# Scores of a head pair as two products over 64 rows and two over 3 rows, in place of one widened product per head

## The chip, the cores and the metric

The kernel runs on one core of one Trainium2 chip. Its time is the device time of one execution in microseconds; a kernel's figure is the median of its runs. One execution was also taken by the hardware profiler, and its trace and page are what this document reads. In them TensorE is PE (matmuls) and PEld (the loads of the stationary operand, which overlap the matmuls), VectorE is DVE, ScalarE is ACT, GpSimd is POOL, and SyncE is SP, which issues most DMAs.

## The reference

Attention in which a query sees only the keys whose nearest centroid is its own, followed by a gated feed-forward block:

```python
# q, k, v: (4, 8, 768, 64); centroids: (8, 16, 64)
q_assign = argmax(einsum('bhsd,hcd->bhsc', q_n, c_n), -1)     # q_n, k_n, c_n: of length 1
k_assign = argmax(einsum('bhsd,hcd->bhsc', k_n, c_n), -1)
mask = q_assign[:, :, :, None] == k_assign[:, :, None, :]
scores = where(mask, q @ k.T / 8, -1e9)
x = softmax(scores) @ v                                        # heads joined: (4, 768, 512)
h = maximum(x @ w_in, 0)                                       # (4, 768, 1024)
gate = sigmoid(conv_w[0]*h[s-1] + conv_w[1]*h[s] + conv_w[2]*h[s+1])
out = (h * gate) @ w_out                                       # float32
```

## The kernel before, in words

The work goes by head pairs: a group `g` is one batch and two heads, so there are 16 groups. A group has two units `t` (the first and the second 384 queries), so there are 32 units. For a group, q and k are loaded in float32 and turned so that the 128 partitions hold the two heads' 64 features each (`qkT`): by PE transposes and copies (`T`, `Qa`, `Qd`) for ten groups, by DVE transposes (`D`) for six. `A` (L318) multiplies by the centroids: four products of 32 output columns each, one per quarter of PE's columns, twice over. `M0` to `M6` are the seven DVE steps of the argmax, `K` turns the resulting numbers with a PE transpose (L386), `Bd` or `Ba` copies them out of PSUM, and `BX` sends them by DMA to where the scores read them.

The mask is put into the scores as three extra rows of the product: with u and w the (shifted, sharpened) cluster numbers of key and query, the rows add a term that is 0 where they are equal and very negative where they are not, and the exponential then gives 0. The operand `ext` has, for each head, 64 rows of features, 3 bias rows (`BR`), and zeros up to 128. `zp` and `zd` fill the zeros once for each of the five buffers. Head 1's features lie in partitions 64 to 127 of `qkT` and must get to partitions 0 to 63 of `ext`: for groups 0 to 3 by casts across partitions (`CDa`, `CDp`, `CDd`, 64 rows each), for the others by one cast of 128 rows into `c16` (`CQ`) and two DMAs (`CX`).

A unit has six score steps `S.t.i` (L413): step `i` takes one head and two key tiles of 128, two products of 128x128 by 128x384, into the two PSUM banks of one of two buffers `sc`. The exponential `E.t.i` (L425) reads both banks on ACT in one go. The values `V.t.u` (L444) are 36 products of 65 columns a unit. Then come the normalisation (`NR`, `N`), the turn of x (`X`, `Y`, or `XD` by DMA), and the feed-forward part: `I` (L498), relu `R`, the three taps of the convolution on DVE (`a`, `b`, `c`, L530 and L532), tanh `H` (L560), gate `G` (L569), the output product `O` (L581), and its way out (`F`, `FX`). `_k.n` are n products on zeros ahead of the real work.

The order of everything is written out in one string, `PLAN`; each engine runs its own steps in that order, and an instruction that waits holds up what stands behind it on its engine. The name after `@` is the PSUM bank.

Of the kernel before, what the change touches and what calls it, by code (L numbers as in the profile page):

```python
# [8 lines left out]
F32 = mybir.dt.float32  # L9
# [7 lines left out]
NE = 5  # L17
NHP = 6
NHK = 2
BUFS = {'qk_in': 4, 'qkT': 2, 'c16': 1, 'v_in': 2, 'spk': 2, 'attn': 4, 'x16': 3, 'cnv': 2, 'th': 2, 'hg': 2, 'o_sb': 2, 'w_sb': 1, 'sim': 1, 'eqq': 1, 'val': 1, 'mx': 3, 'best': 3, 'rec': 3}  # L20

PLAN = (
# [842 lines left out]
```

## Time and profile before

| | |
|---|---|
| median of 3 runs | 241.66 us (241.6 to 242.12) |
| the profiled execution | 240.97 us, of which 239.2 us is the span of its instructions |
| PE busy | 228.5 us, 96% |
| PEld busy | 145.5 us, 61% |
| DVE busy | 209.8 us, 88% |
| ACT busy | 209.5 us, 88% |
| POOL busy | 71.0 us, 30% |
| granted TensorE clock | 1.0 in the whole span |

A busy share tells which engine has the least room over the whole span. It does not tell by itself that the engine is the limit, since a matmul's record goes on until its last result is modelled to be written, while the next one has long begun. How close the products follow each other is read from their starts in the timeline.

### The profile page before, as it was taken

The numbers are of one execution on the slowest core, as the hardware profiler recorded it, in microseconds if no ns is written. First come the engines' busy times: TensorE is split into PE (matmuls) and PEld (weight loads), VectorE is DVE, ScalarE is ACT, GpSimd is POOL, SyncE is SP. The second block draws the span as 40 slices with busy tenths as digits, with TensorE's granted clock in tenths as the row PEclk, the third lists the DMA queues.
The fourth block names the chain that finished last, engine by engine and source line by source line (L and its number), as shares of the span: only waits on it lengthen the run. The fifth ranks groups of instructions, "written<-read, shape, count | busy, mean of one in ns | idle before, by whom it ended". The sixth has DMA issues, their size and how long they took to land.

```text
span 239.2 us, 6261 instructions
## 1 busy us (share of the span) xinstructions
PE 228.5 (96%) x2420; PEld 145.5 (61%) x2420; DVE 209.8 (88%) x417; ACT 209.5 (88%) x326; POOL 71.0 (30%) x120
## 2 busy tenths in 40 slices
PE   7889899999999999989999999999999999999993
PEld 6757567676766775645566556655656666665541
DVE  5689677766989999999999999999899999999950
ACT  3757899898999999989999999997999999987841
POOL 7348690974944004360200340007120000000000
PEclk9999999999999999999999999999999999999999
DMA  8966979899995957796578957885491104022233
GB/s 153 217 154 171 292 192 313 268 225 230 267 229 164 192 96 140 111 152 135 154 144 148 133 129 167 197 135 102 110 249 38 33 3 175 4 88 88 90 132 132
DMA packets 97481, 36.79 MB, mean 154 GB/s; under 512 B 88745, under 2 KB 91305, under 8 KB 97452
## 3 DMA queue, kind: packets, MB, share of 16 engines
q1 hardware_dynamic: 96524, 36.17, 66.4%
q8 instruction: 19, 0.31, 0.6%
q10 hardware_dynamic: 928, 0.23, 0.5%
q14 instruction: 10, 0.08, 0.1%
HBM read 23.11 MB, written 6.29 MB: 123 GB/s over the span
## 4 chain that ended last, share of the span: by engine, by line
PE 65%; DVE 24%; issue 4%; DMA 3%; SPq 1%; ACT 1%; DVEq 0%; ACTq 0%
PE sc L413 18%; PE flex L581 12%; PE flex L498 11%; PE flex L444 10%; DVE cnv L532 5%; PE flex L277 4%; DVE hg L569 3%; PE flex L318 3%; PE tail L581 3%; DMA qk_in<-in_k_dram 2%; PE tail L498 2%; DVE sim L342 2%; DVE val L357 2%; DVE qkT L285 2%; DVE hpad L513 1%
## 5 line engine op out<-in xcount | busy, mean ns | idle before, releaser
L425 ACT ACTIVATE attn<-sc 128x768 f16<-128x768 f32 x192 | 148.1, 829 | 8.7 <-PE sc L413 7.4
L413 PE MATMUL sc<-ext 128*128 128x384 f16 x384 | 90.4, 325 | 0.3
L532 DVE SCALAR_TENSOR_TENSOR cnv<-hpad,cwcol,cnv 128x768 f16<-128x768 f16 (+2 forms) x72 | 62.4, 890 | 0.1
L444 PEld LDWEIGHTS <-attn 128*128 128x128 f16 x1152 | 50.9, 97 | 17.3 <-issue 2.7
L444 PE MATMUL flex<-v,attn 128*128 128x65 f16 x1152 | 55.0, 193 | 0.4 <-DVE sim L342 0.4
L498 PE MATMUL flex<-xT,w_in 128*128 128x384 f16 x228 | 45.5, 325 | 0.3 <-DVE x L460 0.2
L235 POOL CAST c<-qkT 128x768 f16<-128x768 f32 x21 | 21.4, 1027 | 76.6 <-DVE qkT L285 22.9
L413 PEld LDWEIGHTS <-ext 128*128 128x128 f16 x384 | 31.3, 97 | 20.4 <-issue 7.9
L581 PE MATMUL flex<-w_out,hg 128*128 128x512 f16 x160 | 42.3, 379 | 0.0
L498 PEld LDWEIGHTS <-w_in 128*128 128x128 f16 x256 | 24.1, 97 | 16.2 <-issue 1.0
L569 DVE SCALAR_TENSOR_TENSOR hg<-th,hpad 128x768 f16<-128x768 f32 (+3 forms) x34 | 31.1, 919 | 0.4 <-ACT th L560 0.3
L581 PEld LDWEIGHTS <-hg 128*128 128x128 f16 x192 | 17.7, 98 | 16.2 <-issue 0.6
L560 ACT ACTIVATE th<-cnv 128x768 f32<-128x768 f16 (+2 forms) x30 | 25.9, 864 | 1.2 <-DVE cnv L532 1.0
L235 POOL CAST v<-v_in 128x768 f16<-128x768 f32 x16 | 15.9, 997 | 18.9 <-DMA v_in<-in_v_dram 14.1
L511 ACT ACTIVATE hpad<-flex 128x384 f16<-128x384 f32 x39 | 19.5, 536 | 0.4 <-PE flex L498 0.4
L277 PE MATMUL flex<-id,qk_in 128*128 128x128 f32 x120 | 17.5, 277 | 1.6 <-DMA qk_in<-in_k_dram 0.9
L460 DVE TENSOR_TENSOR x<-flex,rec 128x384 f16<-128x384 f32 x32 | 17.5, 547 | 0.2
L277 PEld LDWEIGHTS flex<-id,qk_in 128*128 128x128 f32 x120 | 13.4, 141 | 4.0 <-issue 1.1
L318 PE MATMUL flex<-qkT,cT 128*32 128x384 f32 x128 | 13.6, 498 | 1.6 <-DVE qkT L285 0.8
L235 DVE COPY qkT<-flex 128x512 f32<-128x512 f32 x15 | 10.1, 686 | 5.4 <-PE flex L277 5.3
L530 DVE TENSOR_SCALAR cnv<-hpad,cwcol 128x768 f16<-128x768 f16 (+2 forms) x36 | 14.5, 411 | 0.3 <-ACT th L560 0.2
L233 ACT ACTIVATE qkT<-flex 128x512 f32<-128x512 f32 x15 | 8.7, 603 | 5.3 <-PE flex L277 5.3
(81 smaller groups left out, 210.2 us busy)
## 6 DMA issues: line engine op xcount, KB each, us to landing
v_in<-in_v_dram SPq DMA_DIRECT2D x16, 384.0 KB, 4.6
ext<-c SPq DMA_DIRECT2D x24, 192.0 KB, 3.2
out_dram<-o_sb SPq DMA_DIRECT2D x9, 512.0 KB, 2.8
qk_in<-in_q_dram SPq DMA_DIRECT2D x20, 192.0 KB, 3.1
qk_in<-in_k_dram SPq DMA_DIRECT2D x9, 384.0 KB
qk_in<-in_k_dram SPq DMA_DIRECT2D x24, 96.0 KB, 2.3
qk_in<-in_q_dram SPq DMA_DIRECT2D x24, 96.0 KB, 3.8
w_sb<-in_moe_w_in_dram SPq DMA_DIRECT2D x4, 512.0 KB, 4.4
```

Of the source, the lines that this page charges most:

```text
L235: (nc.vector if name == "d" else nc.gpsimd).tensor_copy(out=to, in_=src)
L277: nc.tensor.transpose(bank[at][:, P * i : P * (i + 1)], qk_t[g][:, o, P * j : P * (j + 1)], id128[:])
L318: nc.tensor.matmul(bank[at][32 * j : 32 * (j + 1), 0:HS], lhsT=cT32[:, g % NPR, :], rhs=tokens[:, j], start=True, stop=True, skip_group_ch ...
L413: nc.tensor.matmul(s[:, n, 0:HS], lhsT=ext_b[g % NE][:, h, 1, P * (kt + n) : P * (kt + n + 1)], rhs=ext_b[g % NE][:, h, 0, HS * a : HS * ( ...
L425: nc.scalar.activation(attn[t, i // 3][:, kt : kt + 2, :], sc[(6 * t + i) % 2][:, :, 0:HS], AF.Exp, scale=0.125)
L444: nc.tensor.matmul(avp(at)[:, u, 0 : D + 1], lhsT=attn[t, h][:, kt, P * jq : P * (jq + 1)], rhs=v16_b[g % NE][:, h, kt, 0 : D + 1], start= ...
L498: nc.tensor.matmul(bank[at][:, 0:HS], lhsT=w_in16[:, r, 2 * u + f, :], rhs=xT[:, b % 2, r, HS * a : HS * (a + 1)], start=(r == 0), stop=(r ...
L511: nc.scalar.activation(to, src, AF.Relu)
L532: nc.vector.scalar_tensor_tensor(out=cnv, in0=src, scalar=w, in1=cnv, op0=ALU.mult, op1=ALU.add)
L560: nc.scalar.activation(th, cnv_t[key].rearrange("p (f s) -> p f s", s=N), AF.Tanh, scale=0.5)
L569: nc.vector.scalar_tensor_tensor(out=hg_b[b][:, 2 * u + fs.start : 2 * u + fs.stop, lo : lo + N], in0=th, scalar=1.0, in1=hpad(b, u)[:, fs ...
L581: nc.tensor.matmul(bank[at][:, 0:Dm], lhsT=hg_b[b][:, fb, P * tq : P * (tq + 1)], rhs=w_out16[:, fb, :], start=(fb == 0), stop=(fb == NFB ...
```

## The change

A score step now takes both heads and one key tile. It makes four products: two over 64 rows (head 0 in partitions 0 to 63, head 1 in 64 to 127, where the features already lie), then two over the 3 bias rows that add to the same banks (head 0's bias in partitions 0 to 2, head 1's in 64 to 66). Head 0 goes to the first bank of `sc`, head 1 to the second. The columns that come out and the exponentials are as many as before, but `attn` is now one tile for both heads, so `V.t.0` needs all six exponentials of its unit. The features are cast in one go of 128 rows (`CD`), there are no shifts (`CX`), no zero fills, no argmax of a single head; `BX` goes once for each head, 36 partitions each.

```diff
+    bias_b = [const.tile([P, 2, S], F16, name=f"bias{i}") for i in range(NE)]
-    ext_b = [const.tile([P, 2, 2, S], F16, name=f"ext{i}") for i in range(NE)]
+    ext_b = [const.tile([P, 2, S], F16, name=f"ext{i}") for i in range(NE)]
...
     def cast_qk(name, g, o):
-        copy(name, c_t[g][:, o], qkT[g][:, o])
+        copy(name, ext_b[g % NE][:, o], qkT[g][:, o])
-    def shift_qk(g, h):
-        nc.sync.dma_start(ext_b[g % NE][0:D, h], c_t[g][D * h : D * (h + 1)])
...
     def bias_rows(g, h, queue=nc.sync):
+        to = bias_b[g % NE][D * h : D * h + BR].rearrange("r o s -> r (o s)")
+        queue.dma_start(to, spk_t[g][60 * h : 60 * h + 36, :])
...
-    def scores(t, i):
-        h, kt = i // 3, 2 * (i % 3)
-        for n in range(2):
-            nc.tensor.matmul(
-                s[:, n, 0:HS],
-                lhsT=ext_b[g % NE][:, h, 1, P * (kt + n) : P * (kt + n + 1)],
-                rhs=ext_b[g % NE][:, h, 0, HS * a : HS * (a + 1)],
-                start=True,
-                stop=True,
-            )
+    def scores(t, kt):
+        s = sc[(6 * t + kt) % 2]
+        for x, K, first in ((ext_b, D, True), (bias_b, BR, False)):
+            for h in range(2):
+                rows = slice(D * h, D * h + K)
+                nc.tensor.matmul(
+                    s[:, h, 0:HS],
+                    lhsT=x[g % NE][rows, 1, P * kt : P * (kt + 1)],
+                    rhs=x[g % NE][rows, 0, HS * a : HS * (a + 1)],
+                    start=first,
+                    stop=not first,
+                    skip_group_check=True,
+                )
...
-                lhsT=attn[t, h][:, kt, P * jq : P * (jq + 1)],
+                lhsT=attn[t][:, kt, h, P * jq : P * (jq + 1)],
```

`PLAN` is another one throughout. Counted in it, before and now: `CX` 24 and 0; casts of 128 rows of q or k 24 and 32, casts of 64 rows 16 and 0 (on ACT, both widths together, 4 and 7); `BX` 18 and 32; argmax passes 18 (four of them of half width) and 16; `zp` and `zd` 10 and 0; products of `_k` 113 and 118. `BUFS` now has two `attn` tiles of double size instead of four, and three `o_sb` instead of two.

On PE, in the middle of the work, a score step that is followed by a feed-forward product. Before (`ext` is the widened operand, `sc` the score buffer):

```order
L444 MATMUL flex_66<-v_4_104,attn 128x65
L413 LDWEIGHTS ext_96
L413 MATMUL sc_77<-ext_96 128x384
L413 LDWEIGHTS ext_96
L413 MATMUL sc_77<-ext_96 128x384
L498 LDWEIGHTS w_in_84
L498 MATMUL flex_69<-xT,w_in_84 128x384
```

Now (L359 is the score line, L442 the feed-forward line):

```order
L359 LDWEIGHTS ext_98
L359 MATMUL sc_77<-ext_98 128x384
L359 LDWEIGHTS ext_98
L359 MATMUL sc_77<-ext_98 128x384
L359 LDWEIGHTS bias_103
L359 MATMUL sc_77<-bias_103 128x384
L359 LDWEIGHTS bias_103
L359 MATMUL sc_77<-bias_103 128x384
L442 LDWEIGHTS w_in_84
L442 MATMUL flex_66<-xT,w_in_84 128x384
```

The step went from two weight loads and two products of 384 columns to four of each; the two on `ext` use 64 of PE's rows each, the two on `bias` use 3 each, and what stands around them uses all 128.

On DVE, at the start, the first group's argmax. Before (`sim` holds the products with the centroids, `hpack` the numbers of single heads):

```order
L342 STREAM_TRANSPOSE sim_275<-flex2_68 128x384
L345 TENSOR_REDUCE mx_277<-sim_275 128x12
L345 TENSOR_REDUCE mx_279<-sim_275 128x12
L351 TENSOR_TENSOR eqq_281<-sim_275,mx_277 128x192
L357 TENSOR_TENSOR val_283<-eqq_281,iota16_83 128x192
L361 TENSOR_REDUCE best_285<-val_283 128x12
L351 TENSOR_TENSOR eqq_287<-sim_275,mx_279 128x192
L365 TENSOR_SCALAR hpack0_108<-best_285 128x12
```

Now (`pack0` is that of both heads of group 0):

```order
L310 STREAM_TRANSPOSE sim_216<-flex2_68 128x384
L313 TENSOR_REDUCE mx_276<-sim_216 128x24
L317 TENSOR_TENSOR eqq_278<-sim_216,mx_276 128x384
L321 TENSOR_TENSOR val_280<-eqq_278,iota16_83 128x384
L324 TENSOR_REDUCE best_282<-val_280 128x24
L329 TENSOR_SCALAR pack0_110<-best_282 128x2x12
L333 TENSOR_TENSOR pack0_110<-pack0_110 128x4x6
L231 COPY spk_290<-flex0_66 96x128
L310 STREAM_TRANSPOSE sim_333<-flex3_69 128x384
```

The two half passes of group 0 became one pass over both heads, and group 1's pass follows it at once.

More of the change, by code (lines that the diff above doesn't have):

```diff
@@ L18 @@
 NHP = 6
-NHK = 2
-BUFS = {'qk_in': 4, 'qkT': 2, 'c16': 1, 'v_in': 2, 'spk': 2, 'attn': 4, 'x16': 3, 'cnv': 2, 'th': 2, 'hg': 2, 'o_sb': 2, 'w_sb': 1, 'sim': 1, 'eqq': 1, 'val': 1, 'mx': 3, 'best': 3, 'rec': 3}
+NHK = 0
+BUFS = {'qk_in': 4, 'qkT': 2, 'v_in': 2, 'spk': 2, 'attn': 2, 'x16': 3, 'cnv': 2, 'th': 2, 'hg': 2, 'o_sb': 3, 'w_sb': 1, 'sim': 1, 'eqq': 1, 'val': 1, 'mx': 3, 'best': 3, 'rec': 3}
 PLAN = (
[118 rows of a table removed]
[114 rows of a table added]
 )
@@ L221 @@
     pack_b = [const.tile([P, P], F16, name=f"pack{i}") for i in range(NPK)]
-    hpack_b = [const.tile([P, P], F16, name=f"hpack{i}") for i in range(NHK)]
     hpad_b = [const.tile([P, 2, S + 4], F16, name=f"hpad{i}") for i in range(NHP)]
-    qk_t, v_t, qkT, chunk_at, c_t = {}, {}, {}, {}, {}
+    qk_t, v_t, qkT, chunk_at = {}, {}, {}, {}
     sims_at, sim_t, mx_t, eq_t, val_t, turn_at, spk_t = {}, {}, {}, {}, {}, {}, {}
@@ L285, in block_transpose @@
         nc.vector.transpose(qkT_of(g)[:, o, :], qk_t[g][:, o, :])
-    def cast_direct(name, g, h, o):
-        copy(name, ext_b[g % NE][0:D, h, o], qkT[g][D * h : D * (h + 1), o, :])
     def cast_qk(name, g, o):
-        if g not in c_t:
-            c_t[g] = rot.tile([P, 2, S], F16, name="c16", tag="c16", bufs=BUFS["c16"])
-        copy(name, c_t[g][:, o], qkT[g][:, o])
-    def transfer_cast(g, h):
-        nc.gpsimd.dma_start(ext_b[g % NE][0:D, h], qkT[g][D * h : D * (h + 1)])
-    def load_v_cast(g):
-        b, h0 = batch_pair(g)
-        src = v[b, h0 : h0 + 2]
-        to = v16_b[g % NE].rearrange("p h j w -> p (h j) w")[:, :, 0:D]
-        if KIND[g] == "B":
-            nc.gpsimd.dma_start(to, src.rearrange("h (j p) d -> p (h j) d", p=P))
-        else:
-            for h in range(2):
-                nc.gpsimd.dma_start(to[:, J * h : J * (h + 1)], src[h].rearrange("(p j) d -> p j d", j=J))
-    def shift_qk(g, h):
-        nc.sync.dma_start(ext_b[g % NE][0:D, h], c_t[g][D * h : D * (h + 1)])
+        copy(name, ext_b[g % NE][:, o], qkT[g][:, o])
     def cast_v(name, g):
@@ L325, in assign, with argmax @@
             )
-    def argmax(g, h, i):
-        key = g, h
-        n = 2 if h is None else 1
-        G = 12 * n
-        pack = pack_b[g % NPK] if h is None else hpack_b[g]
+    def argmax(g, i):
+        pack = pack_b[g % NPK]
         def shape(x):
-            return x[:, 0 : G * C].rearrange("p (u h c) -> p u h c", h=n, c=C)
-        def sim():
-            x = sim_t[g].rearrange("p (u h c) -> p u h c", h=2, c=C)
-            return x if h is None else x[:, :, h : h + 1]
+            return x[:, 0 : 24 * C].rearrange("p (u c) -> p u c", c=C)
         if i == 0:
@@ L343, in argmax @@
         elif i == 1:
-            mx_t[key] = rot.tile([P, 24], F32, name="mx", tag="mx", bufs=BUFS["mx"])
-            nc.vector.tensor_reduce(
-                out=mx_t[key][:, 0:G].rearrange("p (u h) -> p u h", h=n), in_=sim(), axis=AX.X, op=ALU.max
-            )
+            mx_t[g] = rot.tile([P, 24], F32, name="mx", tag="mx", bufs=BUFS["mx"])
+            nc.vector.tensor_reduce(out=mx_t[g][:], in_=shape(sim_t[g]), axis=AX.X, op=ALU.max)
         elif i == 2:
-            eq_t[key] = rot.tile([P, 24 * C], F16, name="eqq", tag="eqq", bufs=BUFS["eqq"])
@@ L350, in argmax @@
-            mx = mx_t.pop(key)[:, 0:G].rearrange("p (u h) -> p u h", h=n).unsqueeze(3).to_broadcast((P, 12, n, C))
-            nc.vector.tensor_tensor(out=shape(eq_t[key]), in0=sim(), in1=mx, op=ALU.is_equal)
+            eq_t[g] = rot.tile([P, 24 * C], F16, name="eqq", tag="eqq", bufs=BUFS["eqq"])
+            mx = mx_t.pop(g)[:].unsqueeze(2).to_broadcast((P, 24, C))
+            nc.vector.tensor_tensor(out=shape(eq_t[g]), in0=shape(sim_t[g]), in1=mx, op=ALU.is_equal)
         elif i == 3:
-            val_t[key] = rot.tile([P, 24 * C], F16, name="val", tag="val", bufs=BUFS["val"])
@@ L354, in argmax @@
-            iota = iota16[:].unsqueeze(1).to_broadcast((P, G, C))
-            eq = eq_t.pop(key)[:, 0 : G * C].rearrange("p (u c) -> p u c", c=C)
-            val = val_t[key][:, 0 : G * C].rearrange("p (u c) -> p u c", c=C)
-            nc.vector.tensor_tensor(out=val, in0=eq, in1=iota, op=ALU.mult)
-        elif i == 4:
-            mx_t[key] = rot.tile([P, 24], F32, name="best", tag="best", bufs=BUFS["best"])
-            val = val_t.pop(key)[:, 0 : G * C].rearrange("p (u c) -> p u c", c=C)
-            nc.vector.tensor_reduce(out=mx_t[key][:, 0:G], in_=val, axis=AX.X, op=ALU.max)
-        elif i == 5:
-            best = mx_t.pop(key)[:, 0:G].rearrange("p (u h) -> p h u", h=n)
-            first = 24 if h is None else 64 * h + 12
-            nc.vector.tensor_scalar(
-                out=pack[:, first : first + G].rearrange("p (h u) -> p h u", h=n),
-                in0=best,
-                scalar1=-8.5,
-                scalar2=SHARP,
-                op0=ALU.add,
-                op1=ALU.mult,
-            )
-        elif h is None:
-            u = pack[:, 24:48].rearrange("p (h o c) -> p o h c", h=2, o=2)
-            to = pack[:, 0:108].rearrange("p (x y) -> p x y", y=54)[:, :, 0:24]
-            to = to.rearrange("p x (h o c) -> p x h o c", h=2, o=2)[:, :, :, 0, :]
-            nc.vector.tensor_tensor(out=to, in0=u, in1=u, op=ALU.mult)
-        else:
-            u = pack[:, 64 * h + 12 : 64 * h + 24].rearrange("p (o c) -> p o c", o=2)
-            to = pack[:, 64 * h : 64 * h + 60].rearrange("p (x y) -> p x y", y=30)[:, :, 0:J]
-            nc.vector.tensor_tensor(out=to, in0=u, in1=u, op=ALU.mult)
@@ L383, in turn @@
-    def turn(g, h, at):
-        turn_at[g, h] = at
-        pack = pack_b[g % NPK] if h is None else hpack_b[g]
-        nc.tensor.transpose(bank16[at][:, 0:P], pack[:], id16[:])
-    def bias_copy(name, g, h):
-        spk_t[g, h] = rot.tile([P, P], F16, name="spk", tag="spk", bufs=BUFS["spk"])
-        rows = slice(0, 72) if h is None else slice(64 * h, 64 * h + 36)
-        copy(name, spk_t[g, h][rows, :], bank16[turn_at[g, h]][rows, 0:P])
-    def bias_rows(g, h, queue=nc.sync):
-        spk = spk_t.pop((g, h))
-        if h is None:
-            queue.dma_start(ext_b[g % NE][D : D + BR].rearrange("r h o s -> r (h o s)"), spk[0:72, :])
-        else:
-            queue.dma_start(
-                ext_b[g % NE][D : D + BR, h].rearrange("r o s -> r (o s)"), spk[64 * h : 64 * h + 36, :]
-            )
+            val_t[g] = rot.tile([P, 24 * C], F16, name="val", tag="val", bufs=BUFS["val"])
@@ new lines, in argmax @@
+            iota = iota16[:].unsqueeze(1).to_broadcast((P, 24, C))
+            nc.vector.tensor_tensor(out=shape(val_t[g]), in0=shape(eq_t.pop(g)), in1=iota, op=ALU.mult)
+        elif i == 4:
+            mx_t[g] = rot.tile([P, 24], F32, name="best", tag="best", bufs=BUFS["best"])
+            nc.vector.tensor_reduce(out=mx_t[g][:], in_=shape(val_t.pop(g)), axis=AX.X, op=ALU.max)
+        else:
+            u = pack[:, 0:120].rearrange("p (h y) -> p h y", h=2)[:, :, 12:24]
+            if i == 5:
+                best = mx_t.pop(g).rearrange("p (u h) -> p h u", h=2)
+                nc.vector.tensor_scalar(out=u, in0=best, scalar1=-8.5, scalar2=SHARP, op0=ALU.add, op1=ALU.mult)
+            else:
+                to = pack[:, 0:120].rearrange("p (h o y) -> p h o y", h=2, o=2)[:, :, :, 0:J]
+                u = u.rearrange("p h (o c) -> p h o c", o=2)
+                nc.vector.tensor_tensor(out=to, in0=u, in1=u, op=ALU.mult)
@@ L402, with turn, bias_copy @@
+    def turn(g, at):
+        turn_at[g] = at
+        nc.tensor.transpose(bank16[at][:, 0:P], pack_b[g % NPK][:], id16[:])
+    def bias_copy(name, g):
+        spk_t[g] = rot.tile([P, P], F16, name="spk", tag="spk", bufs=BUFS["spk"])
+        copy(name, spk_t[g][0:96, :], bank16[turn_at[g]][0:96, 0:P])
+    def bias_rows(g, h, queue=nc.sync):
+        to = bias_b[g % NE][D * h : D * h + BR].rearrange("r o s -> r (o s)")
+        queue.dma_start(to, spk_t[g][60 * h : 60 * h + 36, :])
     attn, rec_t, x16, x_at, av_at = {}, {}, {}, {}, {}
@@ L406, in slot, with exps @@
         return b, a, pr, b * NPR + pr
-    def scores(t, i):
+    def scores(t, kt):
         b, a, pr, g = slot(t)
-        h, kt = i // 3, 2 * (i % 3)
-        s = sc[(6 * t + i) % 2]
-        for n in range(2):
-            nc.tensor.matmul(
-                s[:, n, 0:HS],
-                lhsT=ext_b[g % NE][:, h, 1, P * (kt + n) : P * (kt + n + 1)],
-                rhs=ext_b[g % NE][:, h, 0, HS * a : HS * (a + 1)],
-                start=True,
-                stop=True,
-            )
-    def exps(t, i):
-        if i % 3 == 0:
-            attn[t, i // 3] = rot.tile([P, J, HS], F16, name="attn", tag="attn", bufs=BUFS["attn"])
-        kt = 2 * (i % 3)
-        nc.scalar.activation(
-            attn[t, i // 3][:, kt : kt + 2, :], sc[(6 * t + i) % 2][:, :, 0:HS], AF.Exp, scale=0.125
-        )
+        s = sc[(6 * t + kt) % 2]
[10 more added lines that the diff above has]
+                )
+    def exps(t, kt):
+        if kt == 0:
+            attn[t] = rot.tile([P, J, 2, HS], F16, name="attn", tag="attn", bufs=BUFS["attn"])
+        nc.scalar.activation(attn[t][:, kt], sc[(6 * t + kt) % 2][:, :, 0:HS], AF.Exp, scale=0.125)
     def split_scores(i):
@@ L465, in normalize @@
         )
-        del attn[t, 0], attn[t, 1]
+        del attn[t]
     def xT_of(t):
@@ L624, in load_weights @@
             queue.dma_start(w_t[i].rearrange("p (f d) -> p f d", f=2), rows.rearrange("(f p) d -> p f d", f=2))
-    def load_weights_cast(i):
-        if i < 4:
-            nc.gpsimd.dma_start(w_in16[:, i].rearrange("p fb f -> p (fb f)"), moe_w_in[P * i : P * (i + 1), :])
-        else:
-            rows = moe_w_out[2 * P * (i - 4) : 2 * P * (i - 3), :]
-            nc.gpsimd.dma_start(w_out16[:, 2 * (i - 4) : 2 * (i - 3)], rows.rearrange("(f p) d -> p f d", f=2))
     def cast_weights(name, i):
@@ L642, in pack_fill @@
     def pack_fill(i):
-        nc.gpsimd.memset(pack_b[i][:, 72:P], 0.0)
-        for r, o in ((0, 1), (2, 0)):
-            nc.gpsimd.memset(
-                pack_b[i][:, 24 * r : 24 * r + 24].rearrange("p (h o c) -> p h o c", h=2, o=2)[:, :, o], -0.5
-            )
-    def hpack_fill(i):
-        nc.gpsimd.memset(hpack_b[i][:], -0.5)
+        nc.gpsimd.memset(pack_b[i][:], -0.5)
     at_of = {}
@@ L703, in setup @@
             pack_fill(i)
-        elif name == "hpk":
-            hpack_fill(i)
         elif name == "v":
             nc.gpsimd.memset(v16_b[i][:, :, :, D : D + 1], 1.0)
-        elif name in ("zp", "zd"):
-            (nc.gpsimd if name == "zp" else nc.vector).memset(ext_b[i].bitcast(F32)[D:P, j], 0.0)
         elif name == "hz":
@@ L730, in setup @@
             load_weights(i, nc.scalar)
-        elif name == "wg":
-            load_weights_cast(i)
         elif name in ("wp", "wd", "wa"):
@@ L764, in step @@
         elif name[0:2] == "CD":
-            cast_direct(name[2], *x)
-        elif name[0:2] == "CQ":
             cast_qk(name[2], *x)
-        elif name == "CX":
-            shift_qk(*x)
-        elif name == "CG":
-            transfer_cast(*x)
-        elif name == "VG":
-            load_v_cast(x[0])
         elif name[0:2] == "CV":
@@ L778, in step @@
         elif name[0] == "M":
-            argmax(x[0], last, int(name[1]))
+            argmax(x[0], int(name[1]))
         elif name == "K":
-            turn(x[0], last, at)
+            turn(x[0], at)
         elif name in ("Bd", "Ba"):
-            bias_copy(name[1], x[0], last)
+            bias_copy(name[1], x[0])
         elif name == "BX":
-            bias_rows(x[0], last)
-        elif name == "BA":
-            bias_rows(x[0], last, nc.scalar)
+            bias_rows(*x)
         elif name == "S":
```

232 rows, old and new, of the table PLAN are left out of this document.

## The prediction

> **What bounds the kernel now.** First the page: busy shares, the strip of 40 slices, the granted clock, the chain.
>
> ```profile
> span 239.2 us, 6261 instructions
> ...
> PE 228.5 (96%) x2420; PEld 145.5 (61%) x2420; DVE 209.8 (88%) x417; ACT 209.5 (88%) x326; POOL 71.0 (30%) x120
> ...
> PE   7889899999999999989999999999999999999993
> ...
> PEclk9999999999999999999999999999999999999999
> ...
> PE 65%; DVE 24%; issue 4%; DMA 3%; SPq 1%; ACT 1%; DVEq 0%; ACTq 0%
> ```
>
> PE is busy in nearly every slice at full clock, and 65% of the chain that ended last lies on it. But a busy PE need not be a full one, since products overlap. So next the windows (busy microseconds and instructions by stage):
>
> ```profile
> 16.00:30.00 14.00, 12.54 (x156) 8.41 (x154) 11.83 (x28) 11.87 (x18) 10.21 (x16) 1.00 0.80 223
> 30.00:80.00 50.00, 49.41 (x586) 33.71 (x587) 40.07 (x92) 46.06 (x68) 30.25 (x52) 1.00 0.91 237
> 80.00:130.00 50.00, 48.76 (x539) 30.92 (x536) 48.99 (x89) 48.28 (x78) 10.52 (x9) 1.00 0.78 133
> 130.00:180.00 50.00, 49.67 (x529) 29.42 (x528) 48.83 (x90) 47.75 (x74) 12.04 (x12) 1.00 0.76 156
> 180.00:230.00 50.00, 49.96 (x461) 30.09 (x459) 48.97 (x89) 45.66 (x76) 0.00 (x0) 1.00 0.19 65
> ```
>
> The columns behind the length are PE, PEld, DVE, ACT, POOL. From 30 to 230 us PE has no record running for 2.2 us of 200. Whether it is full inside its records is told by the starts (start, length, engine, line, count), here in the middle of the work:
>
> ```profile
> 101.65 0.49 PE L413 MATMUL sc<-ext 128*128 128x384 f16 x2
> 101.97 0.81 PE L498 MATMUL flex<-xT,w_in 128*128 128x384 f16 x4
> 102.62 0.73 PE L444 MATMUL flex<-v,attn 128*128 128x65 f16 x18
> 103.20 0.84 PE L413 MATMUL sc<-ext 128*128 128x384 f16 x4
> ```
>
> Two products of 384 columns hold PE from 101.65 to 101.97, 0.16 us each; four more to 102.62, again 0.16; 18 products of 65 columns to 103.20, 0.032 each. Nothing lies between them: the next product starts when the last one's columns are in. DVE and ACT are nearly as full (48.9 and 47.8 of 50 us), so less PE time alone would bring little, but more PE time goes straight into the span. A microsecond added to PE between 30 and 230 us costs about one.
>
> **The products themselves.** A score step is now 2 x 0.16 = 0.32 us of PE. After the change it has four products of 384 columns. The rows above show a product's hold on PE going by its columns (384: 0.16; 65: 0.032), all on 128 rows; that fewer rows would shorten it no row shows, and I take it that they don't. Four in a row would take 0.65. If the two of a pair run at once, since they use different rows of the array and different banks, a step is again 2 x 0.16, plus the offset of the second one's start. The trace has no products on different rows, but it has four on different columns: the products with the centroids.
>
> ```profile
> L318 PE MATMUL flex<-qkT,cT 128*32 128x384 f32 x128 | 13.6, 498 | 1.6 <-DVE qkT L285 0.8 <-DVE qkT L235 0.4 <-ACT qkT L233 0.4
> ...
> 35.31 0.49 PE L413 MATMUL sc<-ext 128*128 128x384 f16 x2
> 35.73 0.85 PE L318 MATMUL flex<-qkT,cT 128*32 128x384 f32 x8
> 36.52 0.34 PE L413 MATMUL sc<-ext 128*128 128x384 f16 x1
> ```
>
> Eight of them, 0.498 each, are through in 0.85, so two sets of four: the second set begins 0.85 - 0.49 = 0.36 behind the first, and the four of a set run together. I take it that products on different rows do so too. The offset inside a pair lies between nothing and the 0.032 of a product with its own weight load; I take 0.01, near the concurrent sets: 384 pairs x 0.01 = 3.8 us (bounds 0 and 12).
>
> **Changing the shape in which the array is used.** This is the term that decides. The rows above hold it: the two score products at 35.31 should be in at 35.31 + 2 x 0.162 = 35.63; the column-wise products start at 35.73, 0.10 late, though PE shows no idle time there. The way back:
>
> ```profile
> 105.39 0.49 PE L318 MATMUL flex<-qkT,cT 128*32 128x384 f32 x1
> 105.81 0.50 PE L413 MATMUL sc<-ext 128*128 128x384 f16 x2
> ```
>
> The last centroid product starts at 105.39 and feeds for about 0.33 us (the 0.36 between sets, less the offsets inside one); the score product should start at 105.72 and starts at 105.81, 0.09 late. So going from the whole array to four column strips costs some 0.09 us, and going back the same, as if the array had to empty first. For rows there is one place, the turn of the convolution's weights, products over 3 rows:
>
> ```profile
> 26.34 0.65 PE L718 MATMUL flex<-id,cw 3*128 3x3 f32 x8 [0.21 <-DVE sim L342]
> 26.79 0.20 PE L718 MATMUL flex<-id,cw 3*128 3x3 f32 x1
> 26.92 0.50 PE L413 MATMUL sc<-ext 128*128 128x384 f16 x2
> ```
>
> Seven starts lie between 26.34 and 26.79, 0.064 each. From the last one to the score product on all rows it is 0.13. So the change of shape costs 0.066 if a 3-row product takes 0.064 anyway, 0.10 if it takes no more than the 0.032 of a 65-column product, and 0.13 at most. The column rows lie between; I take 0.09.
>
> [...]
>
> How often does it change? Counted along PE's order: the kernel before changes shape 34 times (16 centroid blocks in and out, the convolution's weights in and out). The new one has 192 steps, each with a change from 64 rows to 3 rows inside. 34 steps follow another directly (one change back to 64 rows); the others are entered from something else and left to something else. In all 560, so 526 more. 526 x 0.09 = 47.3 us (bounds 0.066: 34.7; 0.13: 68.4). A step that stands alone thus takes about 0.32 + 3 x 0.09 + 2 x 0.01 = 0.61 us.
>
> **What it saves.** None of this touches PE in the stage that it bounds. POOL (30% busy) loses eight zero fills of 0.736 us and the widths of its casts change; SP loses 24 shifts and gets 14 more bias transfers:
>
> ```profile
> L709 POOL MEMSET ext<- 64x768 f32 x8 | 5.7, 736 | 0.5 <-POOLq L849 0.3
> ...
> ext<-c SPq DMA_DIRECT2D x24, 192.0 KB, 3.2
> ```
>
> PE shows no idle time that ends on a shift, so I cost their going at nothing; the cover, PE's own work, grows. The same holds for the two DVE passes saved and for three more casts of 0.84 us on ACT (209.5 + 2.5 is far under a span of 290). `V.t.0` now waits for the unit's last exponential; other PE steps stand ahead of it in the order, so nothing while PE is the late one.
>
> The start differs. The exponentials of the first units:
>
> ```profile
> 17.27 1.49 ACT L425 ACTIVATE attn<-sc 128x768 f16<-128x768 f32 x2
> ...
> 19.98 0.81 ACT L425 ACTIVATE attn<-sc 128x768 f16<-128x768 f32 x1 [0.49 <-PE sc L413]
> 21.03 0.81 ACT L425 ACTIVATE attn<-sc 128x768 f16<-128x768 f32 x1 [0.24 <-PE sc L413]
> 22.39 0.81 ACT L425 ACTIVATE attn<-sc 128x768 f16<-128x768 f32 x1 [0.55 <-PE sc L413]
> ...
> 23.89 1.51 ACT L425 ACTIVATE attn<-sc 128x768 f16<-128x768 f32 x2
> 25.84 4.86 ACT L425 ACTIVATE attn<-sc 128x768 f16<-128x768 f32 x6 [0.44 <-PE sc L413]
> ```
>
> Seven exponentials fill the 8.6 us from 17.27 to 25.84, where 7 x 0.81 = 5.7 would do (six take 4.86 in the last row); PE is stuck there behind the turns of single heads. After the change the first step needs both heads' numbers, and group 1's argmax too (its turn stands ahead of it on PE), so it begins no earlier than about 16 us, as now, but then runs without holes. At most 2.9 us come of that, as far as PE follows; PE had 1.5 us idle between 16 and 30. I take 2 (bounds 0 and 2.9). The end of the kernel (feed-forward alone) is as before: 0.
>
> **The sum,** against the profiled execution's 240.97 us (its span of 239.2 and 1.8 around it; the median of the runs is 0.3% higher, 241.66): 240.97 + 47.3 + 3.8 - 2 = 290.1. I say 290. The bounds together: 240.97 + 34.7 + 0 - 2.9 = 272.8 and 240.97 + 68.4 + 12 - 0 = 321; both extremes at once are unlikely, and if the changes from 64 to 3 rows inside a step were free, it would be 526 - 192 = 334 changes, 30.1 us, 272.9. So 270 to 312.
>
> **The rivals.** First, faster: changing between groupings of rows is free, or nearly, since only the column-wise changes are seen often; pairs run at once. Then PE's total stays, and the start decides: 240.97 - 2.9 = 238.1 at best, with the offsets of 3.8 us 241.9. It decides only where a change costs under 2.9 / 526 = 0.006 us. For it speaks that the row evidence is one place; against it that this place gives at least 0.066. Chance 0.14: 0.06 faster, 0.03 within 0.2%, 0.05 slower.
>
> Second: pairs do not run at once but the array need not empty either. Each step has four products of 0.162 in a row: + 192 x 2 x 0.162 = 62.2, less 2: 301 us. Against it speak the four column strips. Chance 0.05.
>
> Third: both, one after the other and with the emptying: 240.97 + 47.3 + 62.2 - 2 = 348 us. Chance 0.04.
>
> My forecast has the remaining 0.77. The range 270 to 312 holds it and the second rival, some 0.82. Slower: 0.77 + 0.05 + 0.04 + 0.05 = 0.91; 0.2% is about what a measurement of this kernel can tell from no change.
>
> **What would show it.** Right: between the last product of a 64-row pair and the first of a 3-row pair some 0.25 us instead of 0.16, with the two of a pair starting within 0.03 us of each other; ACT's and DVE's shares fall to about 73%, with idle time on ACT that ends on the scores; PE near 97%. Wrong: starts at 0.16 throughout (rival one or, if the two of a pair are 0.16 apart, two). The sum fails if the changes inside a step and those at its edges differ in price, or if ACT, being idle more, lets PE wait for something that I have not seen.

## The result, and the profile after

| | before | changed |
|---|---|---|
| median | 241.63 us (240.96 to 242.12) | 291.28 us (289.99 to 310.32) |
| ratio | | 1.204 (95%: 1.198 to 1.209) |

A second round gave 289.35 us, ratio 1.198 (1.191 to 1.205). The change is 20% slower; 290 had been forecast. The changed kernel's profiled execution lasted 310.32 us and not 291, since in it PE was granted only half its clock for 48 us; the starts that follow are read where the clock is full, and the clock has a part of its own below.

The page after, with the rows that answer to those of before:

```profile
span 308.5 us, 6917 instructions
...
PE 301.4 (98%) x2807; PEld 152.8 (50%) x2807; DVE 205.9 (67%) x407; ACT 221.7 (72%) x327; POOL 53.0 (17%) x89
...
PE   6999999999999999999999999999999999999995
...
PEclk9799555555899999999999999999999999999999
...
PE 94%; DMA 2%; DVE 1%; ACT 1%; SPq 0%; issue 0%; DVEq 0%; ACTq 0%
```

PE now holds 94% of the chain instead of 65%, and DVE and ACT have fallen from 88% each to 67% and 72%. The windows (length, then PE, PEld, DVE, ACT, POOL busy, granted clock) say the same for full clock, 80 to 230 us:

```profile
16.00:30.00 14.00, 13.97 (x151) 8.23 (x149) 9.34 (x22) 10.24 (x16) 2.81 (x5) 1.00 0.71 188
30.00:80.00 50.00, 50.00 (x349) 23.16 (x348) 16.84 (x42) 24.89 (x34) 13.96 (x28) 0.52 0.43 126
80.00:130.00 50.00, 50.00 (x554) 27.11 (x555) 35.48 (x73) 39.57 (x56) 14.56 (x19) 1.00 0.43 100
130.00:180.00 50.00, 49.82 (x513) 24.30 (x515) 40.80 (x73) 42.82 (x66) 7.64 (x9) 1.00 0.62 106
180.00:230.00 50.00, 50.00 (x501) 22.75 (x494) 37.13 (x71) 40.51 (x60) 8.98 (x9) 1.00 0.47 99
```

PE has no idle time left, and the others wait for it: the list of waits (us in total, times, longest) has

```profile
ACT attn L371 <- PE sc L359: 53.1, 100, 2.0
```

where the kernel before had 7.4 us. These shares and this wait are those of the whole trace, with the stretch at half clock in it. A kernel that has one more product of one column a step, which turns out to be free (the control over 64 rows, below), was traced at full clock throughout; it has DVE at 73%, ACT at 77% and 37.3 us of this wait. Where PE's time goes is seen in the starts (start, length, engine, line, count), two score steps between value products:

```profile
120.17 0.35 PE L388 MATMUL flex<-v,attn 128*128 128x65 f16 x6
120.46 0.34 PE L359 MATMUL sc<-ext 64*128 64x384 f16 x2
120.73 0.33 PE L359 MATMUL sc<-bias 3*128 3x384 f16 x2
121.00 0.34 PE L359 MATMUL sc<-ext 64*128 64x384 f16 x2
121.26 0.34 PE L359 MATMUL sc<-bias 3*128 3x384 f16 x2
121.53 0.24 PE L388 MATMUL flex<-v,attn 128*128 128x65 f16 x2
```

Read it from the left. A pair is two products and one row; its length of 0.34 is that of a single product, so the second started with the first (0.003 us behind, the median of the 384 pairs). From pair to pair it is 0.27, where one product's columns take 0.16: 0.10 to 0.11 are lost each time the shape changes from 64 rows to 3, from 3 back to 64, and from 3 to all 128. On the way in, six value products from 120.17 should be through at 120.17 + 6 x 0.032 = 120.36, and the first pair starts at 120.46.

The weight loads tell where in the change the time goes. Here are those of the two pairs from 120.46 on, and below them those of the first two pairs of the run with the padded bias, in which the shape stays the same (its products are shown under that run):

```profile
120.45 0.10 PEld L359 LDWEIGHTS <-ext 64*128 64x128 f16 x2
120.72 0.09 PEld L359 LDWEIGHTS <-bias 3*128 3x128 f16 x2 [0.17 <-issue]
```

```profile
120.97 0.10 PEld L359 LDWEIGHTS <-ext 64*128 64x128 f16 x2
120.98 0.10 PEld L359 LDWEIGHTS <-bias 64*128 64x128 f16 x2
```

Where the shape stays, the bias weights are loaded from 120.98 on, while the pair ahead, begun at 120.97, still feeds; their products start at 121.14. Where it changes, the load itself begins only at 120.72, and its products start with it, at 120.73: over all changes at full clock the load leads its product by 0.004 us in the median. So the 0.10 us is not the duration of the load (0.09 us) that could not be hidden; it lies ahead of the load. That the array empties in it, as the prediction and the expectations take it, is not shown: the trace has the wait and not its cause.

### The profile page after: what moved, and what is told of

It is laid out like the page before. It is cut to its first block, busy times and chain, and to the rows that moved or that the text cites. A ratio compares the mean times of both kernels' runs of the same rounds, so it can differ in the third digit from the quotient of the medians.

```text
span 308.5 us, 6917 instructions
## 1 busy us (share of the span) xinstructions
PE 301.4 (98%) x2807; PEld 152.8 (50%) x2807; DVE 205.9 (67%) x407; ACT 221.7 (72%) x327; POOL 53.0 (17%) x89
## 4 chain that ended last, share of the span: by engine, by line
PE 94%; DMA 2%; DVE 1%; ACT 1%; SPq 0%; issue 0%; DVEq 0%; ACTq 0%
PE sc L359 36%; PE flex L388 15%; PE flex L442 14%; PE flex L525 13%; PE flex L273 6%; PE flex L293 4%; DMA qk_in<-in_q_dram 2%; PE tail L442 2%; PE tail L525 1%; PE flex L419 1%; PE sc L593 1%; PE tail L482 1%; PE flex L337 1%; ACT attn L371 1%; SPq L253 0%; PE flex L593 0%
## 5 line engine op out<-in xcount | busy, mean ns | idle before, releaser
L359 PE MATMUL sc<-ext 64*128 64x384 f16 x384 | 68.7, 354 | 0.1
L359 PE MATMUL sc<-bias 3*128 3x384 f16 x384 | 68.5, 353 | 0.0
L388 PEld LDWEIGHTS <-attn 128*128 128x128 f16 x1152 | 47.0, 102 | 18.6 <-issue 13.7
L442 PE MATMUL flex<-xT,w_in 128*128 128x384 f16 x224 | 46.9, 343 | 0.0
L525 PE MATMUL flex<-w_out,hg 128*128 128x512 f16 x176 | 46.4, 380 | 0.0
L359 PEld LDWEIGHTS <-ext 64*128 64x128 f16 x384 | 18.7, 94 | 42.2 <-issue 35.4
L359 PEld LDWEIGHTS <-bias 3*128 3x128 f16 x384 | 18.3, 92 | 37.1 <-issue 36.8
L442 PEld LDWEIGHTS <-w_in 128*128 128x128 f16 x256 | 22.6, 101 | 18.8 <-issue 8.3
L231 POOL CAST ext<-qkT 128x768 f16<-128x768 f32 x21 | 18.5, 884 | 76.7 <-ACT qkT L229 24.1
L399 DVE RECIPROCAL rec<-flex 128x6 f32<-128x6 f32 x32 | 6.1, 190 | 26.6 <-PE flex L388 26.2
L273 PE MATMUL flex<-id,qk_in 128*128 128x128 f32 x120 | 21.4, 320 | 2.0 <-DMA qk_in<-in_k_dram 1.7
L310 DVE STREAM_TRANSPOSE sim<-flex 128x384 f32<-128x384 f32 x16 | 9.3, 579 | 13.4 <-PE flex L293 11.5
```

The source lines that it names most:

```text
L231: (nc.vector if name == "d" else nc.gpsimd).tensor_copy(out=to, in_=src)
L273: nc.tensor.transpose(bank[at][:, P * i : P * (i + 1)], qk_t[g][:, o, P * j : P * (j + 1)], id128[:])
L359: nc.tensor.matmul(s[:, h, 0:HS], lhsT=x[g % NE][rows, 1, P * kt : P * (kt + 1)], rhs=x[g % NE][rows, 0, HS * a : HS * (a + 1)], start=fir ...
L388: nc.tensor.matmul(avp(at)[:, u, 0 : D + 1], lhsT=attn[t][:, kt, h, P * jq : P * (jq + 1)], rhs=v16_b[g % NE][:, h, kt, 0 : D + 1], start= ...
L442: nc.tensor.matmul(bank[at][:, 0:HS], lhsT=w_in16[:, r, 2 * u + f, :], rhs=xT[:, b % 2, r, HS * a : HS * (a + 1)], start=(r == 0), stop=(r ...
L525: nc.tensor.matmul(bank[at][:, 0:Dm], lhsT=hg_b[b][:, fb, P * tq : P * (tq + 1)], rhs=w_out16[:, fb, :], start=(fb == 0), stop=(fb == NFB ...
```

## The experiments

**The changed kernel again**, to see the lost time at full clock and whether PE waits for something else.

> The changed kernel once more, for a profile at full clock. Theory (the array empties at each change of shape, about 0.10 us each, 526 more of them; the two products of a pair run at once): 290 to 292 us; the first product of a 3-row pair starts 0.26 to 0.27 us behind the last of the 64-row pair, which holds 0.16 of products and 0.10 of change; between 30 and 280 us PE shows next to no idle time. Rival (PE waits for other engines, since the order of the steps is another): idle time on PE that ends on ACT or DVE, some 40 us in all.

Measured: 289.35 us; the executions at full clock took 289.1 to 289.4. That is the first theory's figure. Over the trace's 192 steps the median from the last product of a 64-row pair to the first of the 3-row pair is 0.266 us, and PE shows no wait of the rival's size. (This trace too has a stretch at half clock, of 31 us.) All sums below start from 289.2.

**The bias in the shape of the features.** The bias operand is zero in rows 3 to 63, so that both pairs use 64 rows; the number of products and weight loads stays.

```diff
-        for x, K, first in ((ext_b, D, True), (bias_b, BR, False)):
+        for x, K, first in ((ext_b, D, True), (bias_b, D, False)):
...
+        elif name == "bz":
+            nc.gpsimd.memset(bias_b[i].bitcast(F32), 0.0)
```

> The bias operand is filled with zeros to 64 rows, so that the bias pair uses the array in the same shape as the feature pair; as many products and weight loads as before. Theory (change of shape): 192 changes inside the steps go, 192 x 0.10 = 20 us less than the changed kernel: 271 us (269 to 273); from pair to pair inside a step 0.16 us. Rival (the 0.10 between pairs is the weight load of the next pair, or the sums added to the same bank): nothing changes, 291 us; from pair to pair still 0.26.

Measured: 266.92 us (266.65 to 267.22), ratio 1.106 (1.100 to 1.111) to the kernel before. The starts:

```profile
120.97 0.34 PE L359 MATMUL sc<-ext 64*128 64x384 f16 x2
121.14 0.33 PE L359 MATMUL sc<-bias 64*128 64x384 f16 x2
121.30 0.33 PE L359 MATMUL sc<-ext 64*128 64x384 f16 x2
121.47 0.33 PE L359 MATMUL sc<-bias 64*128 64x384 f16 x2
121.72 0.82 PE L525 MATMUL flex<-w_out,hg 128*128 128x512 f16 x3
```

From pair to pair it is now 0.16 to 0.17, and the last pair still needs 0.25 before products on all rows begin. Counted in the trace, 225 changes went and not the 192 of the expectation: besides those inside the steps, the 33 where one step follows another, as at 121.30 above (335 are left of 560). With them went 22.3 us, 0.10 each. The weight loads and the sums into the same bank are as many as before, so the rival is out. The expected 271 was 4 high: 2 lie in the base (291 instead of 289.2), the 33 changes are worth 3.4, and leaving from 64 rows costs 0.01 less than leaving from 3 (0.255 against 0.264, medians), which is 1.4 more; against that, idle time and other waits on PE came back in part.

**No bias products** (the mask is left out).

```diff
-        for x, K, first in ((ext_b, D, True), (bias_b, BR, False)):
+        for x, K, first in ((ext_b, D, True),):
...
-                    stop=not first,
+                    stop=True,
```

> Leaves out the two bias products of each step (so no key is masked). Theory: 192 x (0.16 of products + 0.10 of change) = 50 us less: 241 us, up to 246 where ACT and DVE, as full as before the change, now make PE wait. The changes at the edges of the steps stay and cost as much as the feature pair saves against the old step. Rival (the changes cost nothing, PE is late for another reason): 192 x 0.16 = 31 us less, 260 us.

Measured: 241.82 us (ratio 1.002, 0.999 to 1.005). 47.4 us went with 192 pairs (31 us) and, again, 225 changes (some 23 us). That this sum is higher than 47.4 fits the part of the theory that lets ACT and DVE hold PE up again: PE has 4.6 us of idle time between 30 and 230 us, where the changed kernel had next to none. What is left is equal to the kernel before, although a step has half its products: the two changes at the edges of a step (0.09 each) eat the other half.

**Both heads from the same rows** (head 1 gets head 0's scores).

```diff
-                rows = slice(D * h, D * h + K)
+                rows = slice(0, K)
```

> Head 1's products read head 0's rows (so both heads of a pair get head 0's scores): the two of a pair use the same rows of the array and can't run at once. Theory (a pair runs at once, its second start 0.003 us behind): each pair takes 0.16 us more, 384 x 0.16 = 61 us: 352 us, starts inside a pair 0.16 apart. Rival (the pairs take turns already, and the changes of shape cost nothing): 291 us.

Measured: 437.1 us, far over the 352. The direction is right and the size is not, and the page says why: the granted clock.

```profile
PEclk8995555555555796555599999855599999999999
```

Where the clock is full, the pairs are as expected; where it is half, all is longer (two places of this kernel's timeline):

```profile
250.13 0.50 PE L359 MATMUL sc<-bias 3*128 3x384 f16 x2
250.56 0.36 PE L388 MATMUL flex<-v,attn 128*128 128x65 f16 x6
...
60.85 0.82 PE L359 MATMUL sc<-bias 3*128 3x384 f16 x2
61.60 0.51 PE L388 MATMUL flex<-v,attn 128*128 128x65 f16 x6
```

At full clock a pair holds PE for 0.43 with the change behind it, 0.17 more than with different rows (0.26). So two products on different rows do run at once, and on the same rows they take turns. At half clock it is 0.75. This trace has 205 us at half clock; if 0.43 us of work take 0.75 in all of them, 87 us are lost, and the profiled execution's 438.7 would be some 351 at full clock, the expected figure (an estimate from these rows).

**One more change of shape.** A product of one column over all 128 rows stands between the two pairs; the control has it over the 64 rows of head 0, in the shape of the pair ahead.

```diff
+            if first:
+                nc.tensor.matmul(s[:, 0, 500:501], lhsT=x[g % NE][0:P, 1, P * kt : P * (kt + 1)],
+                                 rhs=x[g % NE][0:P, 0, 0:1], start=True, stop=True, skip_group_check=True)
```

> The changed kernel with one more product of a single column over all 128 rows between the feature pair and the bias pair (into an unused column of the score buffer). Theory (the array empties at each change of shape): 64 rows to 128 to 3 rows is one change more in each of 192 steps, 192 x (0.10 + 0.03) = 25 us: 316 us. Rival (only the product itself costs): 192 x 0.03 = 6 us: 297 us.

> The control: the same extra product of a single column, over the 64 rows of head 0, in the shape of the pair before it. Theory: no further change of shape, 192 x 0.03 = 6 us: 297 us (294 to 300). Rival (an extra weight load and product break up the concurrent pairs and cost as much in either shape): as with 128 rows, about 316 us.

Measured: 320.77 us (312.5 to 331.38) with 128 rows, 293.1 (289.62 to 308.84) with 64; the spread is the clock's (means of 0.92 to 0.99 and 0.92 to 1.00). At full clock the control took 289.62, and the best of the other, at a mean of 0.989, 312.5. So the extra product over 64 rows is free, which I had not expected (0.03 each). The one over 128 rows costs 21 us by the starts (192 x 0.11); the difference of the two runs is 22.9, of which some 3 are the 6.8 us that this trace spent at half clock (an estimate: from pair to pair 0.44 there against 0.27). That is 0.10 to 0.11 per change. The starts agree. First with 128 rows, then the control:

```profile
120.72 0.34 PE L359 MATMUL sc<-ext 64*128 64x384 f16 x2
120.99 0.18 PE L368 MATMUL sc<-ext 128*128 128x1 f16 x1
121.10 0.33 PE L359 MATMUL sc<-bias 3*128 3x384 f16 x2
```

```profile
120.87 0.34 PE L359 MATMUL sc<-ext 64*128 64x384 f16 x2
121.04 0.16 PE L368 MATMUL sc<-ext 64*128 64x1 f16 x1
121.14 0.34 PE L359 MATMUL sc<-bias 3*128 3x384 f16 x2
```

0.27 + 0.11 against 0.17 + 0.10: with one change the stretch from pair to pair is 0.27, with two 0.38.

**The same in the kernel before**, whose order, tiles and casts are untouched: one product of one column behind each score step, over 64 rows, and a control over 128.

```diff
+        nc.tensor.matmul(s[:, 1, 500:501], lhsT=ext_b[g % NE][0:D, h, 1, P * kt : P * (kt + 1)],
+                         rhs=ext_b[g % NE][0:D, h, 0, 0:1], start=True, stop=True)
```

> The kernel before, with one product of a single column over 64 rows behind each score step (into an unused column of the score buffer); order of steps and all else as before. Theory: two changes of shape more in each of 192 steps, 192 x (0.094 + 0.104 + 0.03) = 44 us: 285 us, a little less where PE had idle time at the start. Rival (the loss of the changed kernel lies in its order of steps and its tiles, not in the shapes): 242 to 248 us.

> The control: the kernel before with the same extra product of a single column over all 128 rows, so no change of shape. Theory: 192 x 0.03 = 6 us more: 247 us (244 to 249). Rival (any extra product of one column behind a step costs what the 64-row one costs): about 285 us.

Measured: 274.35 us (ratio 1.137, 1.131 to 1.143) and 243.92 (1.012, 1.006 to 1.018). The product as such costs 2 to 3 us, the 377 more changes 30.4 (in 7 of the 192 places the shape changed there already). That settles that a change of shape alone slows this kernel, whatever the order. Both are under what I had written, 285 and 247: here too the product's own 0.03 vanishes for the most part into the change, and the kernel before had idle time on PE that takes up some of it. The row of the change:

```profile
119.37 0.50 PE L413 MATMUL sc<-ext 128*128 128x384 f16 x2
119.80 0.17 PE L420 MATMUL sc<-ext 64*128 64x1 f16 x1
119.90 0.24 PE L451 MATMUL flex<-v,attn 128*128 128x65 f16 x2
```

119.37 + 0.32 is 119.69; the 64-row product starts 0.11 later, the value product 0.10 behind that.

**The order without the shapes.** Two products over all 128 rows in each step and no bias, in the changed kernel's order (each head gets the sum of both heads' scores, no key is masked).

```diff
-        for x, K, first in ((ext_b, D, True), (bias_b, BR, False)):
...
+                lhsT=ext_b[g % NE][:, 1, P * kt : P * (kt + 1)],
+                rhs=ext_b[g % NE][:, 0, HS * a : HS * (a + 1)],
```

> The changed kernel's order, casts and transfers, with two products over all 128 rows in each step and no bias products (so both heads get the sum of the two heads' scores, and no key is masked): as much PE time in a step as in the kernel before, 2 x 0.16 us, and no change of shape. The prices measured so far add up to 54 us for the changes and the offsets, and the kernel lost 48; what gave 6 us back is open. Theory C (the idle time that PE had in the kernel before is filled because PE is now the late one by far): with PE's load as before, the idle time is back: 240 to 243 us. Theory D (the new order, one cast, no shifts and fewer DVE passes are worth it by themselves): 235 to 238 us.

Measured: 241.29 us, ratio 0.999 (0.996 to 1.002). This is theory C: one cast, no shifts, no zero fills, fewer DVE passes and the new order are worth nothing that can be measured while PE has as much to do as before. The idle time is back: 2.7 us between 30 and 230, from the windows' PE column.

```profile
30.00:80.00 50.00, 48.75 (x579) 33.53 (x580) 39.60 (x84) 46.39 (x69) 27.43 (x42) 1.00 0.68 189
80.00:130.00 50.00, 48.64 (x527) 30.34 (x526) 48.56 (x92) 49.21 (x78) 7.94 (x8) 1.00 0.65 118
130.00:180.00 50.00, 50.00 (x529) 30.10 (x528) 48.77 (x92) 48.96 (x77) 10.20 (x9) 1.00 0.60 122
180.00:230.00 50.00, 49.88 (x466) 30.01 (x463) 49.34 (x93) 43.70 (x71) 1.74 (x1) 1.00 0.19 62
```

**What halves the clock.** Two theories were left after the runs above: few rows in use (A), or many changes of shape (B). Two kernels with the padded bias tell them apart, one with more changes than the changed kernel, one with the products on the same rows:

> The bias padded to 64 rows, and one product of a single column over all 128 rows between the two pairs: 64 to 128 to 64 rows. It changes shape more often than the changed kernel (700 against 560 times) while every pair uses all 128 rows. Theory on the time: two changes and one product more in each step than with the padding alone, 192 x (0.104 + 0.094 + 0.03 - 0.02 that the one-column product saves at the edge) = 40 us on 267: 307 us. On the granted clock, theory A (the clock is halved where the products use few rows of the array): full clock in every run, as with the padding alone. Theory B (it is halved where the array is emptied often): stretches at 0.5 as in the changed kernel, and more of them.

> Head 1's products read head 0's rows, as in the run whose clock fell to half for long stretches, with the bias padded to 64 rows (both heads get head 0's scores). One shape within a step, 316 changes in all; every product uses 64 rows, one after the other. Time at full clock: 267 + 384 x 0.17 = 332 us. On the granted clock, theory A (few rows): 64 rows all the time instead of 64 and 3, so at least far fewer stretches at 0.5 than the 0.77 mean of that run, above 0.95. Theory B (emptying): also above 0.95, since changes are as few as with the padding alone; if it still falls to about 0.77, both fall.

Measured: 306.98 us (ratio 1.270, 1.264 to 1.275), as expected to the microsecond, at a mean clock of 0.999 to 1.000 in all four executions. And 327.21 us (1.355, 1.349 to 1.361) at 0.995 to 1.000, where the same kernel with 3-row products had 0.77. So 719 changes of shape did not lower the clock. Theory A stands for this kernel: the long stretches at half clock came with the 3-row products. Of the 20 executions of kernels that have them (the changed one, same rows, one more column), 13 had a mean clock under 0.99; of all other kernels, none did. How few rows are too few, and whether zeros in the padded rows play a part, no run here tells.

None of these kernels is faster than the one before.

## Why the prediction was right, point by point

- **PE bounds the kernel, and time added to it is added to the span.** Right: PE has 94% of the chain, and of some 54 us that were added, 48 came in the time. The small addition to the kernel before, one column over 128 rows a step, came in part: 2.8 us of some 5 (192 x 0.028, by the starts), since PE had idle time there.
- **The two of a pair run at once.** Right; the offset was over-sized: 0.003 us and not 0.01, so 384 pairs cost 1.2 us and not 3.8.
- **The price of a change of shape.** This decided. That each change costs time, inside the steps and at their edges, was right; the size was a little low. From the starts (medians less the 0.162 from one product of 384 columns to the next): 64 rows to 3, 0.103; 3 rows to 64 or to 128, 0.102; 128 to 64, 0.094. With the order's counts, 192 x 0.103 + (34 + 159) x 0.102 + 158 x 0.094, and 17 centroid or other changes at 0.09 to 0.10, that is 56.0 us, and 3.2 for the 34 of before: 52.8 more, where I had 47.3. (The 560 changes are in the trace; of the 34 from 3 rows to 64, 33 are steps that follow another and one follows the convolution's turn.) I had taken the column-wise price of 0.09; the one row-wise place, bounded by 0.066 and 0.13, was nearer to the truth in its middle.
- **The start.** Wrong. I put the first step at 16 us, as before, and gave a gain of 2. This is the changed kernel with the free one-column product, at full clock. The last step of group 1's argmax on DVE, its turn and the first score step on PE:

```profile
17.36 0.17 DVE L333 TENSOR_TENSOR pack<-pack 128x24 f16<-128x24 f16 x1
17.73 0.22 PE L337 MATMUL flex<-id,pack 128*128 128x128 f16 x1
17.88 0.34 PE L359 MATMUL sc<-ext 64*128 64x384 f16 x2
```

The prediction names this turn as standing ahead of the first step, and gave it no time; the step starts at 17.88 behind it, where it was 16.10 before. The exponentials on ACT follow, two in a row each:

```profile
18.53 1.51 ACT L380 ACTIVATE attn<-sc 128x768 f16<-128x768 f32 x2 [0.27 <-PE sc L359]
20.32 1.74 ACT L380 ACTIVATE attn<-sc 128x768 f16<-128x768 f32 x2 [0.28 <-PE sc L359]
22.38 1.51 ACT L380 ACTIVATE attn<-sc 128x768 f16<-128x768 f32 x2 [0.31 <-PE sc L359]
24.77 1.52 ACT L380 ACTIVATE attn<-sc 128x768 f16<-128x768 f32 x2
```

The first begins at 18.53 instead of 17.27, and they are held up by the scores, so the eighth begins at about 25.5, where it began at 25.84 before: next to no gain.

- **What came back instead.** The terms as measured are 241.4 + 52.8 + 1.2 = 295.4, and the kernel takes 289.2. Of the 6.2 us between, the windows show some 3.5 as idle time of PE that has gone (16 to 30 us: 1.5 before, none now; 30 to 230: 2.2 before, 0.2 in the 150 us at full clock). The order without the shapes shows that it is not the saved work as such that gave it. Waits during which a record of PE still runs show as no idle time, but they show in the starts, as the 0.10 us ahead of 120.46 does, where the record of the last value products runs to 120.52. What lies between the starts of two products beyond the columns of the first, summed over the trace and without the price of the changes, is some 13 us in the kernel before and some 8 in the changed kernel with the free product: 5 us less, idle time included. Some 1 us stays open.
- **So the total was nearer than its terms, and that part is luck.** The changes were 5.5 too low, the offsets 2.6 too high, and the 2 us at the start, which did not come, stand against 6 of waits that went elsewhere and that the sum did not have.
- **What did not matter:** shifts, fills, casts and DVE passes, costed at nothing. Right by the order without the shapes.
- **The rivals.** Free changes: out, by the starts. Pairs in turn: out, by the run on the same rows. The halved clock was in none of them; in executions at full clock it plays no part.

## What to carry to other kernels

Before a full-height product is split over parts of the array, count how often the shape changes along PE's order and price it with a place in the trace where it already changes: here 0.1 us each, against 0.16 us for a product of 384 columns. Products that belong together did better here in one shape, even at the price of zeros: padding 3 rows to 64 gave back 22 of the 48 us. That also made steps that follow each other free of a change between them (33 of the 225 changes that went), so steps of one shape are best put next to each other. Work that was saved on engines with cover brought nothing here, as the order without the shapes shows (241.3 against 242.0).

## What the hardware showed that was not expected

PE's granted clock fell to half for stretches of 7 to 113 us in kernels with the 3-row products, while PE had work without a gap. Short stretches are not tied to these products: one of 3.4 us at the start, from 7.4 us on, stands in the trace without bias products as well, and means down to 0.990 occur in the kernel before. In both traces of the changed kernel the long stretch begins at 31.4 to 31.5 us. In the first one's profile, two windows of equal length (PE busy throughout, clock 0.50 and 1.00):

```profile
31.50:79.00 47.50, 47.50 (x325) 22.07 (x323) 15.59 (x38) 23.01 (x31) 13.96 (x28) 0.50 0.42 126
80.00:127.50 47.50, 47.50 (x534) 25.90 (x532) 32.98 (x70) 37.57 (x53) 13.91 (x18) 1.00 0.44 103
```

325 products at half clock, 534 at full. It came in some executions of one kernel and not in others (289.1 to 310.3 us for the changed one). In the window at 0.50 PE was busy for 47.50 of 47.50 us, so busy time by the records did not by itself keep the clock up. With the bias padded to 64 rows no execution fell below a mean of 0.995 (12 of them).

A product of one column in the shape of the one ahead of it cost nothing where a change of shape followed it: 289.6 us with 192 of them against 289.2 without, both at full clock.
